# A recurrent attention in chunks: the state held compact, one head on each half of the partitions, and the output in two PSUM banks

## The chip, the cores and the metric

The kernel runs on one core of a Trainium2 chip. Five engines of that core work side by side, each in its own program order: PE (matrix multiplication), with its weight loads shown apart as PEld; DVE (elementwise and reductions); ACT (activations, copies); POOL (elementwise, slower); SP (issues DMAs). PE writes only to PSUM, which has eight banks of 2 KB in each of 128 partitions. An engine waits for another by a semaphore, and whatever stands behind the waiting instruction in its program order waits too.

The metric is the time of one execution on the device in microseconds (us), as the median over runs.

## The reference

Two parts follow one another. The first is a recurrent attention over 768 steps for 4 batches and 8 heads of 48 channels. The second routes the 3072 resulting rows through 8 experts, with weights from a gate that is normalised eight times over rows and columns (Sinkhorn).

```python
state = zeros(B, H, D, D)                         # B, H, S, D = 4, 8, 768, 48
for t in range(S):
    kt, vt, rt = k[:, :, t], v[:, :, t], r[:, :, t]
    cur = einsum('bhd,bhe->bhde', u[None] * kt, vt)
    y[:, :, t] = einsum('bhd,bhde->bhe', rt, state + cur)
    state = w[None, :, :, None] * state + einsum('bhd,bhe->bhde', kt, vt)

x = y as (3072, 384)
P = exp(x @ w_gate - max); eight times: rows of P to sum 1, columns of P to sum N / E
out = sum over e of P[:, e] * (relu(x @ w1[e]) @ w2[e])
```

## The kernel before

The time axis is cut into chunks of 128 steps. There are 24 chunks (`NTT`), six to a batch (`NCHB`); chunk `tt` is number `c = tt % 6` of its batch, and the state is zero ahead of `c = 0`. Within a chunk the recurrence is written as matrix products. r and k are first scaled by powers of the decay w (`rp`, `kp`), transposed on PE (`prT`, `pkT`) and copied by ACT to `rT`, `kT`, with the eight heads as four pairs: head 2p on partitions 0 to 47, head 2p+1 on 64 to 111, the other partitions zero. Then:

- `stage_c`: `pA` = kT times rT for each head, in two PSUM tiles, one for each head of a pair, on quarters of 64x64 of the array. DVE copies the part above the diagonal to `at` with a masked copy (`COPY_PREDICATED`), one for each tile.
- `stage_s` (for c < 5): `pu` = kp times v, the chunk's contribution to the state, on columns of the array 32 wide. DVE adds the old state, POOL multiplies by the chunk's decay `wbd`; for c = 0 DVE multiplies alone. The result is the state of the next chunk.
- `stage_d`: `py` = rT times state (the state part, for c > 0) plus `at` times v. DVE adds the bonus term `av` (the tile `rk`), which gives `x`, and takes the row's greatest value and a scale from it.

The state `S` is a tile of [128, 4 pairs, 2, 48]: for each pair a block of 128 x 96 in which the even head's state stands in the upper left and the odd head's in the lower right; the other two quarters are zero, set once at the start. So one product of 128 rows and 96 columns gives both heads of a pair:

```python
for p_ in range(NPAIR):
    for hs in quarters:
        T.matmul(
            pyp[hs, p_, :], d["rT"][:, p_, hs], d["S"][:, p_].rearrange("p j d -> p (j d)"),
            start=first, stop=False, skip_group_check=True,
        )
```

A product in fp32 runs as two passes, so each call leaves two records in the trace.

The main loop runs over `i` from 0 to 26. Iteration i makes the scaled r and k of chunk i+2 (`prep`), the transposes of chunk i+1 (`stage_b`), `stage_c` and `stage_s` of chunk i, `stage_d` of chunk i-1, the gate's logits of chunk i-3 (`px`, then `lparts`). Between them stand fixed numbers of units of the first expert's products (`ph`, `po`) as soon as these are ready, for i < 5 a few matmuls on zeros (`pz`), and small steps that split weights and combine tokens on DVE, ACT and POOL (`prepare`, `n_steps`). Every engine is kept in the order in which the code issues (`InOrder`, line 29, which is why all lines read L29).

`prT`, `pkT`, the two `pA`, `pu` and `py` share one pool of four PSUM banks (`ps3`, tag "pa"). Each new tile takes over the bank of the tile four places earlier in the order of allocation, and its first matmul waits until that tile has been read. With six tiles in an iteration, `prT` and `pkT` of chunk i+2 take over the banks of the two `pA` of chunk i, and `pu` that of a `prT`. After the attention (near 226 us) the rest of the experts follows, PE almost without a break.

Of the kernel before, what the change touches and what calls it, by code (L numbers as in the profile page):

```python
# [8 lines left out]
F32 = mybir.dt.float32  # L9
# [3 lines left out]
ALU = mybir.AluOpType  # L13
# [19 lines left out]
def rwkv_sinkhorn_moe(  # L33
# [13 lines left out]
    V, S_, G, T, Q = (  # L47
        InOrder(tc, e) for e in (nc.vector, nc.scalar, nc.gpsimd, nc.tensor, nc.sync)
    )

    B, H, S, D = r.shape
    NT, DM = out.shape
    E, _, F = w1.shape
    P = 128
    C = 128
    NPAIR = H // 2
    NCHB = S // C
    NTT = NT // P
# [5 lines left out]
    HP = 64  # L64
    QP = 32
# [63 lines left out]
    def pow2_scale(m, inv, s, down):  # L129
        V.tensor_scalar(inv, m, 1e-30, down, op0=ALU.max, op1=ALU.mult)  # L130
        V.tensor_single_scalar(
            inv.bitcast(I32), inv.bitcast(I32), EXP_MASK, op=ALU.bitwise_and
        )
        V.reciprocal(s, inv)
# [137 lines left out]
    ac = att.enter_context(tc.tile_pool(name="ac", bufs=1))  # L272
    ld = att.enter_context(tc.tile_pool(name="ld", bufs=3))
    at2 = att.enter_context(tc.tile_pool(name="at2", bufs=2))
    ps3 = att.enter_context(tc.tile_pool(name="ps3", bufs=4, space=PSUM))
# [13 lines left out]
    def spin(n):  # L289
        pz = ps2.tile([P, TB], F32, tag="po", name="pz")  # L290
        for _ in range(n):
            T.matmul(pz, zeros[:, :P], zeros, start=True, stop=True)
# [52 lines left out]
    def fill(x_):  # L345
        n = x_.shape[1]
        S_.mul(
            x_.rearrange("p (a q) -> p a q", q=HP),
            unit[:, :1, 1:].broadcast_to([P, n // HP, HP]), 0.0,
        )  # L350

    fill(hbx[:, 2 * HB :])
    spin(19)
    wbd = ac.tile([P, NPAIR, 2, D], F32, name="wbd")
    G.memset(wbd, 0.0)

    mask = ac.tile([P, C], F32, name="mask")
    G.memset(mask, 1.0)
# [7 lines left out]
    kp_ = [ac.tile([P, H, HP], F32, name=f"kp{i}") for i in range(3)]  # L366
    at_ = [ac.tile([P, H, C], F32, name=f"at{i}") for i in range(2)]

    ss_ = [ac.tile([P, NPAIR, 2, D], F32, name=f"S{i}") for i in range(3)]
    for t_ in rp_ + kp_:  # L370
        G.memset(t_[:, :, D:], 0.0)
    for t_ in ss_:
        for j in range(2):
            G.memset(t_[j * HP : (j + 1) * HP, :, 1 - j, :], 0.0)
    fill(at_[0].rearrange("p h c -> p (h c)"))

    rk0 = at2.tile([P, H, D], F32, tag="rk", name="rk_0", bufs=3)
# [88 lines left out]

    wc = ac.tile([P, NPAIR], F32, name="wc")
    V.tensor_tensor(wc, pw[:, :, HP], pw[:, :, HP], op=ALU.mult)
    for j in range(2):
        rows = slice(j * HP, j * HP + D)  # L470
        V.tensor_copy(wbd[rows, :, j, :], wc[rows].unsqueeze(2).broadcast_to([D, NPAIR, D]))
    iswg = ac.tile([P, 1], F32, name="iswg")
    swg = ac.tile([P, 1], F32, name="swg")
    wgm = ac.tile([P, 1], F32, name="wgm")
# [3 lines left out]
    def gate_max():  # L478
        V.tensor_reduce(wgm, wg, axis=AX.XY, op=ALU.max, apply_absolute_value=True)
# [11 lines left out]
    st = {}  # L491
# [4 lines left out]
    def prep(tt):  # L496
        ld_ = loads[tt]
        G.tensor_tensor(rp_[tt % 2][:, :, :D], ld_["r"], rt4, op=ALU.mult)
        V.tensor_tensor(kp_[tt % 3][:, :, :D], ld_["k"], kt4, op=ALU.mult)
        st[tt] = {}  # L500
# [49 lines left out]
    def stage_s(tt):  # L550
        d = st[tt]
        c = tt % NCHB
        if c < NCHB - 1:
            vn = loads[tt]["v"]
            kp = kp_[tt % 3].rearrange("p (a j) d -> p a (j d)", j=2)

            pu = ps3.tile([P, NPAIR, D], F32, tag="pa", name=f"pu_{tt}")
            for p_ in range(NPAIR):
                for q in range(0, P, QP):
                    T.matmul(  # L560
                        pu[q : q + QP, p_, :], kp[:, p_, q : q + QP],
                        vn[:, 2 * p_ + q // HP, :], start=True, stop=True,
                    )
            sn = ss_[tt % 3]
            for j in range(2):
                rows = slice(j * HP, (j + 1) * HP)
                if c == 0:
                    V.tensor_tensor(sn[rows, :, j, :], pu[rows], wbd[rows, :, j, :], op=ALU.mult)
                else:
                    V.tensor_tensor(sn[rows, :, j, :], pu[rows], d["S"][rows, :, j, :], op=ALU.add)  # L570
            if c:
                for j in range(2):
                    rows = slice(j * HP, (j + 1) * HP)
                    G.tensor_tensor(
                        sn[rows, :, j, :], sn[rows, :, j, :], wbd[rows, :, j, :], op=ALU.mult
                    )
            st.setdefault(("S", tt + 1), sn)

    def stage_d(tt):
        d = st[tt]  # L580
        c = tt % NCHB
        vn = loads[tt]["v"]
        at = at_[tt % 2]
        py = ps3.tile([P, H, D], F32, tag="pa", name=f"py_{tt}")
        pyp = py.rearrange("p (a j) d -> p a (j d)", j=2)

        quarters = [slice(q, q + QP) for q in range(0, P, QP)]
        first = True
        if c > 0:
            for p_ in range(NPAIR):  # L590
                for hs in quarters:
                    T.matmul(
                        pyp[hs, p_, :], d["rT"][:, p_, hs], d["S"][:, p_].rearrange("p j d -> p (j d)"),
                        start=first, stop=False, skip_group_check=True,
                    )
                first = False
        for h in range(H):
            for hs in quarters:
                T.matmul(
                    py[hs, h, :], at[:, h, hs], vn[:, h, :],  # L600
                    start=first, stop=(h == H - 1), skip_group_check=True,
                )
            first = False
        x = at2.tile([P, DM], F32, tag="x", name=f"x_{tt}")
        V.tensor_tensor(x, py.rearrange("p h d -> p (h d)"), d["av"].rearrange("p h d -> p (h d)"), op=ALU.add)
        m = at2.tile([P, 1], F32, tag="xm", name=f"xm_{tt}")
        V.tensor_reduce(m, x, axis=AX.X, op=ALU.max, apply_absolute_value=True)
        s = at2.tile([P, 1], F32, tag="xs", name=f"xs_{tt}")
        pow2_scale(m, inv_s[:, tt : tt + 1], s, 0.125)
        d["x"], d["s"] = x, s  # L610
# [8 lines left out]
    def stage_e(tt):  # L619
        Q.dma_start_transpose(xtile(tt), st[tt]["x"].rearrange("p l d -> p (l d)"))  # L620
# [130 lines left out]
    def n_steps(i):  # L751
        return STEPS.get(i, (2, 2) if i < 22 else (3, 2))
# [5 lines left out]
    for i in range(NTT + 3):  # L758
        if i == 1:
            gate_max()  # L760
        if i + 2 < NTT:
            prep(i + 2)
        if i + 1 < NTT:
            bonus_dot(i + 1)
        if i + 1 < NTT and i:
            stage_b(i + 1)
        if 2 <= i <= NTT + 1:
            scale_x(i - 2)
            stage_e(i - 2)
            emitted[0] = i - 1  # L770
        if i + 4 < NTT:
            load_part(i + 4, "r", r)
            load_part(i + 4, "k", k)
            if i == 0:
                load_part(4, "v", v)
                Q.dma_start(raws[1], w2[0].rearrange("(c p) d -> p c d", p=P))
        work(1, i > 4)
        if i < NTT:
            bonus(i)
            if ("S", i) in st:  # L780
                st[i]["S"] = st.pop(("S", i))
            stage_c(i)
            stage_s(i)
        if i == 2:
            gate_split(gate_res)
        if i == 0:
            stage_b(1)
        if i > NTT:
            work(2)
        for _ in range(n_steps(i)[0] if i < 5 else 0):  # L790
            prepare()
        if 1 <= i <= NTT:
            stage_d(i - 1)
            if i + 4 < NTT:
                load_part(i + 4, "v", v)
        for _ in range(n_steps(i)[0] if i >= 5 else 0):
            prepare()
        if 3 <= i:
            stage_f(i - 3, ps2.tile([P, TB], F32, tag="po", name=f"px_{i}"))
        if i <= NTT:  # L800
            work(2 if i > 8 else 1, i > 4)
        if i == 1:
            gate_res = gate_across()
        for _ in range(n_steps(i)[1]):
            prepare()
        done = i - 2
        if 0 <= done < NTT and done % TH == TH - 1:
            po_ = done // TH
            if po_ == 0:
                units += [g1_unit(0, fc, W) for fc in range(FC)]  # L810
                units += [g2_half(0, t, 0, W) for t in range(TH)]
                pend = [(0, t, 1) for t in range(TH)]
            for j in range(2 if po_ else 0):
                g1 = [g1_unit(po_, fc, W) for fc in range(j * FHC, (j + 1) * FHC)]
                g2 = [g2_half(*a, W) for a in pend]
                units += merged(g1, g2)
                pend = [(po_, t, j) for t in range(TH)]
# [151 lines left out]
    _, singles2, _, high2, low2 = early[2]  # L969
# [249 lines left out]
    for s in range(NS):  # L1219
        tasks = stage_tasks(s)  # L1220
        for g in range(NG):
            for j in range(2):
                for n, nxt in enumerate(g1_slots(s, g, j)):
# [3 lines left out]
                    i = j * NPR + n  # L1227
# [37 lines left out]
```

## Time and profile before

| what | value |
|---|---|
| median of 3 runs | 1535.79 us (1535.17, 1535.79, 5633.4) |
| the profiled execution: its own time | 1534.0 us |
| its span, first to last instruction | 1532.5 us |
| mean granted PE clock | 0.997 |
| 0 to 88 us: PE, DVE, POOL busy | 70.5, 80.1, 68.8 us; clock 0.96 |
| 88 to 226 us: PE, DVE, POOL busy | 136.0, 119.1, 124.1 us of 138; clock 0.99 |
| 226 us to the end: PE, DVE, POOL busy | 1301.6, 834.1, 404.6 us of 1306.5; clock 1.00 |

One of the three runs took 5633.4 us; the median does not see it. In the profile, "PE prT <- DVE at: 4.7, 3, 3.2" means that PE stood idle ahead of work on prT until DVE had done something with at: 4.7 us in all, 3 times, 3.2 at the longest. A group's line gives the engine, the operation, output <- inputs, the tile of the array, the shape, the count, then busy us and the mean ns of one. Of matmuls that run side by side on parts of the array the busy time counts the overlap once. In the timeline, records of one kind that follow each other are merged: start, length from the first start to the last end, count, and in brackets the idle time before and what ended it.

### The profile page before, as it was taken

How to read it: one execution, taken by the hardware profiler on the slowest of the kernel's cores; microseconds unless marked ns; L12 is line 12 of the kernel's file. 1: busy time of each engine (PE TensorE's matmuls, PEld its weight loads, DVE VectorE, ACT ScalarE, POOL GpSimd, SP SyncE). 2: the span in 40 equal slices, each digit the busy share in tenths (PEclk: the TensorE clock that was granted, in tenths of full speed). 3: DMA queues.
4: the chain of work that ended last, by engine and by line, in shares of the span. 5: the costliest groups of instructions: out<-in, count | busy, mean ns of one | idle time of the engine just before them, and what ended most of it. 6: DMA issues, size and time to landing. Idle time of an engine off the chain costs nothing.

```text
span 1532.5 us, 29056 instructions
## 1 busy us (share of the span) xinstructions
PE 1508.2 (98%) x11721; PEld 850.5 (55%) x11721; DVE 1033.3 (67%) x1714; ACT 662.2 (43%) x1168; POOL 597.5 (39%) x708
## 2 busy tenths in 40 slices
PE   7899999999999999999999999999999999999999
PEld 4667766655555555555555555555555555555555
DVE  8988887676666666667666666656666566566564
ACT  4333434435354444535454444535344444445320
POOL 8779995120213425242424334242424224242200
PEclk9999999999999999999999999999999999999999
DMA  9665623121235665665656665655445554555433
GB/s 203 96 112 116 134 58 109 47 76 52 98 57 107 91 115 86 126 94 91 107 90 128 92 123 80 127 62 98 59 67 86 60 98 57 99 59 99 57 93 130
DMA packets 186859, 143.31 MB, mean 94 GB/s; under 512 B 109537, under 2 KB 180962, under 8 KB 186722
## 3 DMA queue, kind: packets, MB, share of 16 engines
q0 software_dynamic: 44928, 61.36, 32.4%
q1 hardware_dynamic: 141584, 80.07, 20.2%
q8 instruction: 92, 1.51, 0.4%
q14 instruction: 45, 0.37, 0.1%
q10 hardware_dynamic: 210, 0.00, 0.0%
HBM read 55.39 MB, written 80.23 MB: 88 GB/s over the span
## 4 chain that ended last, share of the span: by engine, by line
PE 92%; DVE 5%; POOL 1%; issue 1%; ACT 0%; DMA 0%; DVEq 0%; POOLq 0%; another core or an unknown queue 0%; ACTq 0%
PE po L29 48%; PE bZ L29 12%; PE bY L29 12%; PE bA L29 5%; PE ph L29 5%; PE bB L29 5%; PE bC L29 2%; PE py L29 1%; PE pA L29 1%; POOL rk L29 1%; DVE at L29 1%; DVE hb L29 1%; DVE ws L29 0%; PE prT L29 0%; PE pu L29 0%
## 5 line engine op out<-in xcount | busy, mean ns | idle before, releaser
L29 PE MATMUL po<-ws,hbx 128*128 128x384 f16 x3360 | 736.8, 326 | 0.0
L29 POOL DMA_DIRECT2D accd<-stg x288 | 250.0, 868 | 695.0 <-ACT stg L29 676.5
L29 PEld LDWEIGHTS <-hbx 128*128 128x128 f16 x3504 | 334.2, 98 | 292.9
L29 PEld LDWEIGHTS <-ws 128*128 128x128 f16 x3096 | 302.0, 98 | 245.6 <-issue 3.0
L29 ACT ACTIVATE hbx<-tb 128x512 f16<-128x512 f32 x224 | 141.0, 630 | 450.7 <-DVE tb L29 450.7
L29 PE MATMUL po<-ws,hb 128*128 128x384 f16 x1248 | 323.4, 326 | 3.6 <-DVE ws L29 2.3
L29 DVE TENSOR_TENSOR tb<-bY,tb 128x512 f32<-128x512 f32 x168 | 116.2, 692 | 195.6 <-PE bY L29 195.4
L29 ACT ACTIVATE stg<-po,pe 128x384 f32<-128x384 f32 x312 | 179.4, 575 | 121.8 <-PE po L29 98.7
L29 PE MATMUL bZ<-xv,ws 128*128 128x512 f16 x840 | 227.0, 379 | 0.7 <-DVE tb L29 0.7
L29 PE MATMUL bY<-xv,ws 128*128 128x512 f16 x840 | 227.0, 379 | 0.0
L29 DVE TENSOR_TENSOR tb<-bZ,tb 128x512 f32<-128x512 f32 x168 | 115.5, 688 | 136.5 <-PE bZ L29 136.5
L29 PEld LDWEIGHTS <-hb 128*128 128x128 f16 x1248 | 121.4, 98 | 97.2 <-issue 4.2
L29 POOL TENSOR_TENSOR ucb<-rawb 128x256 f32<-128x256 f32 x84 | 75.9, 954 | 118.5 <-DMA rawb<-in_moe_w_dram 118.5
L29 DVE TENSOR_TENSOR tb<-bB,tb 128x512 f32<-128x512 f32 x112 | 77.5, 692 | 48.8 <-PE bB L29 46.9
L29 PE MATMUL ph<-hbx,ws 128*128 128x384 f16 x576 | 105.1, 328 | 0.6 <-DVE hb L29 0.6
L29 DVE SCALAR_TENSOR_TENSOR hb<-tb,hbx 128x512 f16<-128x512 f32 x112 | 77.1, 689 | 24.7 <-ACT hbx L29 19.5
L29 PE MATMUL bA<-xv,ws 128*128 128x512 f16 x336 | 90.8, 379 | 0.0
L29 PE MATMUL bB<-xv,ws 128*128 128x512 f16 x336 | 90.8, 379 | 0.0
L29 DVE SCALAR_TENSOR_TENSOR hbx<-tb,hbx 128x512 f16<-128x512 f32 x112 | 78.2, 698 | 14.7 <-ACT hbx L29 10.4
L29 ACT ACTIVATE hb<-ph 128x384 f16<-128x384 f32 x64 | 31.3, 491 | 73.9 <-PE ph L29 73.5
L29 ACT COPY tb<-bZ 128x512 f32<-128x512 f32 x56 | 32.8, 586 | 65.5 <-PE bZ L29 65.5
L29 ACT COPY stg<-po 128x384 f32<-128x384 f32 x48 | 22.9, 478 | 75.7 <-PE po L29 60.5
(166 smaller groups left out, 1537.7 us busy)
## 6 DMA issues: line engine op xcount, KB each, us to landing
accd<-stg POOLq DMA_DIRECT2D x288, 192.0 KB, 3.7
rawb<-in_moe_w_dram SPq DMA_DIRECT2D x28, 768.0 KB, 7.0
e0d<-stg SPq DMA_DIRECT2D x48, 192.0 KB, 2.1
hb<-e0d SPq DMA_DIRECT2D x48, 192.0 KB, 3.7
vn<-in_v_dram SPq DMA_DIRECT2D x24, 192.0 KB, 4.2
accd<-stg SPq DMA_DIRECT2D x24, 192.0 KB, 1.8
accd<-hb POOLq DMA_DIRECT2D x24, 192.0 KB, 4.8
rawb<-accd SPq DMA_DIRECT2D x24, 192.0 KB, 2.4
```

What stands on the lines that cost most here:

```text
L29: return lambda *a, **k: self.tc.keep_in_program_order(f(*a, **k))
```

## The change

Four edits go together.

1. The state tile becomes [128, 4 pairs, 48]: the even head's state on partitions 0 to 63, the odd head's on 64 to 127, without the zero quarters. `wbd` shrinks likewise. The additions and multiplications of the state, two over 64 partitions each, become one over 128. The memsets of the zero quarters and of `wbd` go.
2. The state part of y (`state_part`, new) runs on quarters of 64x64 of the array, 48 columns each, where it ran on 128x32 with 96 columns. The number of matmuls stays 16 in a chunk.
3. y stands in two PSUM tiles, `py_0` for the even and `py_1` for the odd heads, each of [128, 4, 48]. The addition that makes x becomes two.
4. `stage_s` of chunk i moves behind `stage_d` of chunk i-1; the state part comes straight behind `stage_c`.

```diff
-    wbd = ac.tile([P, NPAIR, 2, D], F32, name="wbd")
-    G.memset(wbd, 0.0)
+    wbd = ac.tile([P, NPAIR, D], F32, name="wbd")
...
-    ss_ = [ac.tile([P, NPAIR, 2, D], F32, name=f"S{i}") for i in range(3)]
+    ss_ = [ac.tile([P, NPAIR, D], F32, name=f"S{i}") for i in range(3)]
...
-    for t_ in ss_:
-        for j in range(2):
-            G.memset(t_[j * HP : (j + 1) * HP, :, 1 - j, :], 0.0)
...
-    for j in range(2):
-        rows = slice(j * HP, j * HP + D)
-        V.tensor_copy(wbd[rows, :, j, :], wc[rows].unsqueeze(2).broadcast_to([D, NPAIR, D]))
+    V.tensor_copy(wbd, wc.unsqueeze(2).broadcast_to([P, NPAIR, D]))
...
             sn = ss_[tt % 3]
-            for j in range(2):
-                rows = slice(j * HP, (j + 1) * HP)
-                if c == 0:
-                    V.tensor_tensor(sn[rows, :, j, :], pu[rows], wbd[rows, :, j, :], op=ALU.mult)
-                else:
-                    V.tensor_tensor(sn[rows, :, j, :], pu[rows], d["S"][rows, :, j, :], op=ALU.add)
-            if c:
-                for j in range(2):
-                    rows = slice(j * HP, (j + 1) * HP)
-                    G.tensor_tensor(
-                        sn[rows, :, j, :], sn[rows, :, j, :], wbd[rows, :, j, :], op=ALU.mult
+            if c == 0:
+                V.tensor_tensor(sn, pu, wbd, op=ALU.mult)
+            else:
+                V.tensor_tensor(sn, pu, d["S"], op=ALU.add)
+                G.tensor_tensor(sn, sn, wbd, op=ALU.mult)
+            st.setdefault(("S", tt + 1), sn)
+
+    def y_banks(tt):
+        return [ps3.tile([P, NPAIR, D], F32, tag="pa", name=f"py_{tt}_{g}") for g in range(2)]
+
+    def state_part(tt):
+        d = st[tt]
+        if tt % NCHB == 0:
+            return
+        d["py"] = y_banks(tt)
+        for p_ in range(NPAIR):
+            for g in range(2):
+                rows = slice(g * HP, (g + 1) * HP)
+                for hs in (slice(0, HP), slice(HP, C)):
+                    T.matmul(
+                        d["py"][g][hs, p_, :], d["rT"][rows, p_, hs], d["S"][rows, p_, :],
+                        start=(p_ == 0), stop=False, skip_group_check=True,
...
+        pys = d["py"] if "py" in d else y_banks(tt)
         for h in range(H):
-            for hs in quarters:
+            for q in range(0, P, QP):
                 T.matmul(
-                    py[hs, h, :], at[:, h, hs], vn[:, h, :],
-                    start=first, stop=(h == H - 1), skip_group_check=True,
+                    pys[h % 2][q : q + QP, h // 2, :], at[:, h, q : q + QP], vn[:, h, :],
+                    start=(c == 0 and h < 2), stop=(h >= H - 2), skip_group_check=True,
...
-        V.tensor_tensor(x, py.rearrange("p h d -> p (h d)"), d["av"].rearrange("p h d -> p (h d)"), op=ALU.add)
+        xv = x.rearrange("p (a g d) -> p g a d", g=2, d=D)
+        av = d["av"].rearrange("p (a g) d -> p g a d", g=2)
+        for g in range(2):
+            V.tensor_tensor(xv[:, g], pys[g], av[:, g], op=ALU.add)
...
             stage_c(i)
-            stage_s(i)
+        if 1 <= i <= NTT:
+            state_part(i - 1)
...
             stage_d(i - 1)
+        if i < NTT:
+            stage_s(i)
+        if 1 <= i <= NTT:
```

What the change does to the order is seen on PE around chunk 14 (iteration 14). The names carry running numbers; pA_1 is the second of the two tiles of stage_c, py's inputs are S with rT (the state part) or vn with at, and px belongs to the gate. On PE before, from the last pA on:

```order
L29 MATMUL pA_1_2582<-rT_2375,kT_2382 64x128 x2
L29 MATMUL pu_2601<-vn_1972,kp_170 32x48 x16
L29 MATMUL py_2622<-S_173,rT_2192 32x96 x16
L29 MATMUL py_2622<-vn_1781,at_172 32x48 x32
L29 LDWEIGHTS hbx
L29 MATMUL px_2681<-wgp,hbx 128x16
```

On PE now, first the start of the state part behind the last pA, with the engines that an instruction waits for:

```order
L29 MATMUL pA_1_2579<-rT_2372,kT_2379 64x128 x2
L29 MATMUL py_0_2598<-S_172,rT_2188 64x48 [waits Activation_49]
L29 MATMUL py_0_2598<-S_172,rT_2188 64x48
L29 MATMUL py_1_2599<-S_172,rT_2188 64x48 [waits Activation_49]
L29 MATMUL py_1_2599<-S_172,rT_2188 64x48
```

and then the end of y, with pu:

```order
L29 MATMUL py_1_2599<-vn_1775,at_171 32x48 x4
L29 MATMUL pu_2657<-vn_1966,kp_169 32x48 [waits DVE_49]
L29 MATMUL pu_2657<-vn_1966,kp_169 32x48 x15
L29 LDWEIGHTS hbx [waits DMAHW2_49,DMASW3_49]
L29 MATMUL px_2678<-wgp,hbx 128x16
```

pu has moved from ahead of y to behind it, and it waits for DVE. With seven tiles in an iteration, pu takes over the bank of the same chunk's first pA, which DVE's masked copy reads; pkT of chunk i+2 takes over that of py_0.

On DVE, chunk 13 before; at is what the masked copies write, and x, xm, inv_s, xs are the output, its greatest value and its scale:

```order
L29 COPY_PREDICATED at_172<-mask,pA_0_2408 128x4x128
L29 COPY_PREDICATED at_172<-mask,pA_1_2409 128x4x128
L29 TENSOR_TENSOR S_174<-pu_2428,S_173 64x4x48 x2
L29 TENSOR_TENSOR x_2482<-py_2449,rk_2016 128x384
L29 TENSOR_REDUCE xm_2484<-x_2482 128x1
```

and now:

```order
L29 COPY_PREDICATED at_171<-mask,pA_0_2405 128x4x128
L29 COPY_PREDICATED at_171<-mask,pA_1_2406 128x4x128
L29 TENSOR_TENSOR x_2459<-py_0_2425,rk_2010 128x4x48
L29 TENSOR_TENSOR x_2459<-py_1_2426,rk_2010 128x4x48
L29 TENSOR_REDUCE xm_2462<-x_2459 128x1
L29 TENSOR_SCALAR inv_s<-xm_2462 128x1
L29 TENSOR_SCALAR inv_s<-inv_s 128x1
L29 RECIPROCAL xs_2464<-inv_s 128x1
L29 TENSOR_TENSOR S_173<-pu_2468,S_172 128x192
```

The state's addition has moved from ahead of x to behind x's scale, and there are two additions for x and one for the state.

More of the change, by code (lines that the diff above doesn't have):

```diff
@@ L564, in stage_s @@
             sn = ss_[tt % 3]
-            for j in range(2):
-                rows = slice(j * HP, (j + 1) * HP)
-                if c == 0:
-                    V.tensor_tensor(sn[rows, :, j, :], pu[rows], wbd[rows, :, j, :], op=ALU.mult)
-                else:
-                    V.tensor_tensor(sn[rows, :, j, :], pu[rows], d["S"][rows, :, j, :], op=ALU.add)
-            if c:
-                for j in range(2):
-                    rows = slice(j * HP, (j + 1) * HP)
-                    G.tensor_tensor(
-                        sn[rows, :, j, :], sn[rows, :, j, :], wbd[rows, :, j, :], op=ALU.mult
+            if c == 0:
[18 more added lines that the diff above has]
+                        start=(p_ == 0), stop=False, skip_group_check=True,
                     )
-            st.setdefault(("S", tt + 1), sn)
     def stage_d(tt):
@@ L583, in stage_d @@
         at = at_[tt % 2]
[L584 to L590, printed above, removed]
-                for hs in quarters:
[L592 to L596, printed above, removed]
+        pys = d["py"] if "py" in d else y_banks(tt)
         for h in range(H):
-            for hs in quarters:
+            for q in range(0, P, QP):
                 T.matmul(
-                    py[hs, h, :], at[:, h, hs], vn[:, h, :],
-                    start=first, stop=(h == H - 1), skip_group_check=True,
+                    pys[h % 2][q : q + QP, h // 2, :], at[:, h, q : q + QP], vn[:, h, :],
+                    start=(c == 0 and h < 2), stop=(h >= H - 2), skip_group_check=True,
                 )
-            first = False
         x = at2.tile([P, DM], F32, tag="x", name=f"x_{tt}")
-        V.tensor_tensor(x, py.rearrange("p h d -> p (h d)"), d["av"].rearrange("p h d -> p (h d)"), op=ALU.add)
+        xv = x.rearrange("p (a g d) -> p g a d", g=2, d=D)
+        av = d["av"].rearrange("p (a g) d -> p g a d", g=2)
+        for g in range(2):
+            V.tensor_tensor(xv[:, g], pys[g], av[:, g], op=ALU.add)
         m = at2.tile([P, 1], F32, tag="xm", name=f"xm_{tt}")
```

## The prediction, on record before the changed kernel ran

> **What bounds the kernel now.** I read the page first, then the busy time by stretches, then the groups by shape, and last the timeline of single chunks on PE, DVE and ACT. The page's head gives the span and the share of each engine:
>
> ```profile
> span 1532.5 us, 29056 instructions
> PE 1508.2 (98%) x11721; PEld 850.5 (55%) x11721; DVE 1033.3 (67%) x1714; ACT 662.2 (43%) x1168; POOL 597.5 (39%) x708
> ```
>
> PE is idle for 24 us of the whole span, so almost anything that PE saves or loses shows at the end. Where the idle time lies is seen in the stretches (busy us and instructions of PE, PEld, DVE, ACT, POOL, then the granted clock):
>
> ```profile
> 40.00:60.00 20.00, 16.22 (x386) 11.49 (x379) 19.50 (x36) 4.62 (x9) 15.39 (x17) 0.89 0.51 94
> 60.00:80.00 20.00, 17.21 (x457) 12.81 (x459) 18.12 (x45) 9.63 (x17) 13.87 (x16) 1.00 0.80 110
> 80.00:100.00 20.00, 16.77 (x321) 11.82 (x309) 18.70 (x34) 5.29 (x11) 12.47 (x14) 0.91 0.52 109
> 100.00:120.00 20.00, 20.00 (x462) 14.64 (x464) 15.20 (x32) 7.39 (x15) 19.38 (x22) 1.00 0.81 126
> 500.00:1000.00 500.00, 500.00 (x2734) 267.37 (x2733) 329.43 (x502) 239.65 (x422) 184.85 (x223) 1.00 0.64 104
> ```
>
> Two regimes: until about 88 us DVE is busy 18 to 19.5 of 20 us and sets the pace, while PE waits; from 100 us PE is full. The attention ends near 226 us, and the change touches nothing behind that. PE's waits in the first regime, with their last releaser (us, times, longest):
>
> ```profile
> PE prT L29 <- DVE at L29: 4.7, 3, 3.2
> PE po L29 <- DVE ws L29: 2.3, 1, 2.3
> PE prT L29 <- POOL rp L29: 0.5, 1, 0.5
> ```
>
> The second row is the last large one. So the change is worth two things: what it does to DVE before 88 us, and what it does to PE in the later chunks.
>
> **The state part.** One chunk on PE, in order of time, then the groups by shape that the change edits:
>
> ```profile
> 154.45 1.10 PE L29 MATMUL pA<-rT,kT 64*64 64x128 f32 x32
> 155.48 0.55 PE L29 MATMUL pu<-vn,kp 128*32 128x48 f32 x32
> 155.84 0.84 PE L29 MATMUL py<-S,rT 128*32 128x96 f32 x32
> 156.50 0.89 PE L29 MATMUL py<-vn,at 128*32 128x48 f32 x64
> 157.33 0.30 PE L29 MATMUL px<-wgp,hbx 128*128 128x16 f16 x6
> ...
> L29 PE MATMUL py<-S,rT 128*32 128x96 f32 x640 | 17.9, 255 | 0.0
> L29 DVE TENSOR_TENSOR x<-py,rk 128x384 f32<-128x384 f32 x24 | 13.3, 555 | 1.2 <-PE py L29 0.7
> L29 DVE TENSOR_TENSOR S<-pu,S 64x192 f32<-64x192 f32 x32 | 11.1, 347 | 0.5
> L29 POOL TENSOR_TENSOR S<-S,wbd 64x192 f32<-64x192 f32 x32 | 21.7, 679 | 1.2
> ```
>
> From start to start, the state part takes 156.50 - 155.84 = 0.66 us: 32 records, four at a time, 8 steps of 82 ns for 96 columns. pu, with 48 columns, takes 0.36 us, 45 ns a step. The new state part also has 32 records, four at a time, of 48 columns, but on tiles of 64x64 as pA has. From below it costs what pu does, 0.36. From above: pA takes 1.03 us, 129 ns a step for 128 columns; taking off 80 columns at (82-45)/48 = 0.77 ns leaves 67 ns, 0.54 us; and if 64-wide loads set the pace whatever the columns, 1.03 us stays. I take 0.42, nearer to pu because its shape in columns is the same: 0.24 us saved a chunk (0.30 to 0.12, or 0.37 lost). By the Trainium skill (TensorEngine Tiling (Array Packing), Instruction Overhead) a matmul with fewer than about 60 columns costs what one of 60 does; by that the part would take 0.66 x 60/96 = 0.41 us and save 0.25, and the 45 ns of pu against 82 (0.55, not 0.62) do not show such a floor.
>
> 20 of the 24 chunks have a state part, which PE does one iteration later. Those of chunks 1 to 5 and 7 lie before 88 us, where PE has time to spare; there it gains nothing. 14 remain.
>
> **DVE.** The two state additions of a chunk become one over 128 partitions with the same 192 elements each: 0.35 us less. The output's addition becomes two of 192 elements. No row has 128x192 from PSUM; the nearest is 64x192 at 0.35, so 2 x 0.35 against 0.555: 0.15 more (0 to 0.2). Before 88 us there are 8 of each: -8 x 0.35 + 8 x 0.15 = -1.6 us, and that moves the point where PE is let go. Bounds: -2.8 if the halves cost nothing more, and 0 if PE's own later waits fill the time.
>
> **POOL and start.** Sixteen pairs of multiplications by the decay become single ones, some 0.6 us less each, but POOL now gets them later, since the state addition stands behind the output's scale on DVE. PE waits for POOL only 0.5 us in all (the row above), and the state is needed one iteration later, so zero; if that cover went, POOL's order would put rp late by one such wait. The dropped memsets and one copy lie ahead of waits that stay:
>
> ```profile
> POOL rp L29 <- ACT rtab L29: 3.8, 1, 3.8
> DVE kp L29 <- ACT ktab L29: 1.2, 1, 1.2
> ```
>
> Zero as well. PE's work in the new order (y, then pu) has the same changes of tile shape as before.
>
> **The new wait.** A chunk now takes seven PSUM tiles out of four banks where it took six. The bank of pu is therefore the one that pA's first half had, and pu cannot start before DVE has done the first masked copy of the same chunk (the order shows pu waiting for DVE, before for ACT). Before, PE went on past pu, y, px and one or two units of expert work until the next prT. Now only the state part and the rest of y (0.42 + 0.83 us) stand between pA and that wait; behind pu queue px, the units and the next transposes, all of PE. In chunks where DVE is late this costs at once. Chunk 13, and chunk 19, which is built alike (both follow a chunk with zero state, so there is no state part between):
>
> ```profile
> 127.13 1.10 PE L29 MATMUL pA<-rT,kT 64*64 64x128 f32 x32
> 128.17 0.55 PE L29 MATMUL pu<-vn,kp 128*32 128x48 f32 x32
> 128.53 0.86 PE L29 MATMUL py<-vn,at 128*32 128x48 f32 x64
> 129.33 0.30 PE L29 MATMUL px<-wgp,hbx 128*128 128x16 f16 x6
> 134.67 2.11 PE L29 MATMUL po<-ws,hb 128*128 128x384 f16 x12 [0.74 <-DVE lparts L29]
> ...
> 125.32 0.83 ACT L29 CAST xv<-ws 128x768 f16<-128x768 f32 x1
> 126.19 1.11 DVE L29 TENSOR_TENSOR xv<-ws,xv 128x768 f16<-128x768 f32 x1 [1.96 <-ACT xv L29]
> 130.72 1.34 DVE L29 COPY_PREDICATED at<-mask,pA 128x512 f32<-128x512 int32 x2
> ...
> 182.22 0.55 PE L29 MATMUL pu<-vn,kp 128*32 128x48 f32 x32
> 182.59 0.86 PE L29 MATMUL py<-vn,at 128*32 128x48 f32 x64
> 183.38 0.30 PE L29 MATMUL px<-wgp,hbx 128*128 128x16 f16 x6
> 184.63 1.35 DVE L29 COPY_PREDICATED at<-mask,pA 128x512 f32<-128x512 int32 x2
> ```
>
> In chunk 13 PE would reach pu at 128.17 + 0.80 = 128.97; the first of the two copies ends at 130.72 + 0.67 = 131.39: 2.4 us. DVE is late there because a cast on ACT came late (the 1.96), and the cast follows PE's own work, so the lateness moves with PE. The wait takes over the 0.74 at 134.67, so net 1.7. In chunk 19: 182.22 + 0.79 = 183.01 against 184.63 + 0.68 = 185.31, 2.3 us. Chunk 12 shows the other kind:
>
> ```profile
> 119.31 0.55 PE L29 MATMUL pu<-vn,kp 128*32 128x48 f32 x32
> 119.84 1.39 DVE L29 COPY_PREDICATED at<-mask,pA 128x512 f32<-128x512 int32 x2
> ```
>
> PE at 119.31 + 0.42 + 0.82 = 120.55, the copy done at 120.54: no wait, but no slack either, so in such a chunk a shorter state part only waits. I therefore count the 0.24 in 8 of the 14 chunks: -1.9 us. The waits of the other chunks behind 13 and 19 I put at 0.8, between 0 (PE is already late by then) and 1.7 (one more net wait like chunk 13's).
>
> **Sum.** -1.6 - 1.9 + 1.7 + 2.3 + 0.8 = +1.3 us. The profiled execution took 1534.0 us (span 1532.5, and 1.5 around it); that makes 1535.3. The median of the three runs shown is 1535.79, 1.8 above it; in its terms 1537.1, rounded to 1537.
>
> **The rivals.**
> - The wait doesn't bite. DVE does 0.2 us less in each chunk and may run early enough, then only the gains stay: 1535.8 - 1.6 - 14 x 0.24 = 1530.8, and 1528.8 with both low prices (2.8 and 14 x 0.30). For it: DVE has 15.2 of 20 us at 100. Against it: chunk 13's lateness comes from ACT, not from DVE's load.
> - The wait is paid nearly everywhere (slower). If every second of the 20 pu's pays chunk 13's 2.4 us, 24 less the gains of 3.5 gives 1556; from 15 of them on it is past 2% ((30.7 + 3.5) / 2.4 = 14.3). For it: DVE is nearly full in 80 to 100 us. Against it: chunk 12, and that a PE that waited once comes later the next time.
> - The clock. After a wait of 3.19 us PE ran slow; a unit of 9 that takes 1.63 us took 2.68:
>
> ```profile
> 50.64 0.72 PE L29 MATMUL prT<-ident,rp 128*128 128x128 f32 x4 [3.19 <-DVE at L29]
> 52.30 2.68 PE L29 MATMUL ph<-hbx,ws 128*128 128x384 f16 x9
> 59.92 1.63 PE L29 MATMUL ph<-hbx,ws 128*128 128x384 f16 x9
> ```
>
>  The stretch 80 to 100 with a mean clock of 0.91 lost 0.09 x 20 = 1.8 us. One or two such stretches behind chunks 13 and 19 make 1539 to 1541. The Trainium skill (TensorE: Matmul & The Clock Gate, Part 1: The HAM clock gate) says that the clock halves after an idle window of about 3.4 us that runs free of the kernel. By that rule my waits of 2.4 us may or may not fall so, which the trace neither shows nor excludes.
> - The tiles of 64x64 don't get shorter with fewer columns (the change doesn't do what it says): 14 x 0.37 = 5.2 lost, and with the waits' 4.8 less the 1.6 of DVE 8.4 in all, 1544.
>
> **How the numbers follow.** Forecast 0.35, no bite 0.25, the clock 0.20, paid widely 0.12, long tiles 0.08. About 2% (30.7 us) is what a measurement of this kernel can tell from no change; only the end of the widely paid case passes it, 0.02, and on the fast side the gains together stay far below it, 0.01. So 0.97 for within 2%. The range runs from 1529, the low end of the first rival, to 1546, which cuts off most of the widely paid case: some 0.15 left out, beside what I have not thought of.
>
> **What would show it.** The groups: py<-S at 64x48 with about 9 us busy instead of 17.9; S additions 20, x additions 48, at about 0.35 us each. The waits: pu <- DVE at, in chunks 13 and 19 above 2 us. The stretches: PE no longer full in 120 to 140 and 180 to 200, and let go before 88 us. It would be wrong if pu shows no wait, if a stretch behind 226 us changes, or if the copies move with PE in most chunks.

## The result and the profile after

| | changed kernel | kernel before |
|---|---|---|
| median | 1543.92 us (5 runs, 1542.9 to 1547.83) | 1535.61 us (5 runs, 1535.17 to 1535.79 and one of 5633.4) |
| profiled execution: its own time, span | 1543.92, 1542.4 us | 1534.0, 1532.5 us |
| ratio | 1.0066, 95% interval 1.0055 to 1.0077 | |

So the change made the kernel 0.66% slower, about 8 us: within 2%, inside the range, 7 us above the forecast of 1537.0. The head of the page of the changed kernel:

```profile
span 1542.4 us, 29007 instructions
PE 1509.8 (98%) x11721; PEld 850.3 (55%) x11721; DVE 1029.0 (67%) x1717; ACT 661.3 (43%) x1168; POOL 584.8 (38%) x685
```

PE is busy as long as before, within 2 us; the span is 10 us longer, so most of the loss is idle time of PE. Where it lies is seen in the stretches of the changed kernel (columns as in the prediction: busy us and instructions of PE, PEld, DVE, ACT, POOL, then granted clock, where 1.00 is full speed, DMA share, GB/s):

```profile
120.00:140.00 20.00, 17.53 (x379) 12.64 (x379) 15.20 (x29) 7.22 (x14) 17.99 (x19) 1.00 0.46 94
140.00:160.00 20.00, 17.91 (x428) 13.06 (x416) 18.33 (x37) 6.76 (x13) 12.27 (x13) 1.00 0.61 124
...
180.00:200.00 20.00, 16.52 (x329) 11.53 (x327) 13.53 (x25) 7.14 (x14) 17.03 (x20) 0.91 0.43 96
200.00:220.00 20.00, 18.21 (x307) 12.42 (x311) 15.04 (x32) 6.78 (x13) 9.47 (x11) 0.91 0.21 41
```

Before, PE was busy 19.26, 20.00, 20.00 and 19.30 us in these four, at a clock of 1.00. Now 9 to 17% of a stretch is idle, and the last two ran at a mean clock of 0.91, which is 1.8 us lost in each (0.09 x 20). From 226 us to the end PE idled 4.9 us before and idles 4.5 us now, at a clock of 1.00 in both. PE's waits in the changed kernel (us, times, longest) name one releaser:

```profile
PE pu L29 <- DVE at L29: 20.9, 14, 2.5
...
PE prT L29 <- DVE at L29: 0.5, 1, 0.5
```

The wait of prT that stood at 4.7 us has gone to pu and has grown more than fourfold. On PE's timeline of the changed kernel, pu with its idle time in brackets, and the units of expert work behind it:

```profile
130.86 0.55 PE L29 MATMUL pu<-vn,kp 128*32 128x48 f32 x32 [2.47 <-DVE at L29]
...
188.12 0.85 PE L29 MATMUL pu<-vn,kp 128*32 128x48 f32 x32 [2.00 <-DVE at L29]
189.09 2.85 PE L29 MATMUL ph<-hbx,ws 128*128 128x384 f16 x9
...
200.42 0.55 PE L29 MATMUL pu<-vn,kp 128*32 128x48 f32 x32 [1.89 <-DVE at L29]
201.06 3.26 PE L29 MATMUL po<-ws,hb 128*128 128x384 f16 x12
204.12 2.20 PE L29 MATMUL ph<-hbx,ws 128*128 128x384 f16 x9
```

130.86 is chunk 13, 188.12 chunk 19, 200.42 chunk 20. A unit of nine matmuls (`ph`) takes 1.63 us elsewhere and 2.85 behind chunk 19's wait; a unit of twelve (`po`) takes 2.11 elsewhere and 3.26 behind chunk 20's: two stretches at half clock (the granted clock is 0.50 from 189 to 191 and from 202 to 205 us), which the kernel before does not have behind 100 us. The waits of chunks 14, 15 and 16 were 1.36, 0.56 and 0.43 us, so behind 100 us there are 8.7 us of such waits, and within chunk 21's pu PE waits 1.37 us more for something that the profile does not name. The other 12.2 of the 20.9 us lie ahead of 100 us. What they do there is seen at the start of pA in chunk 12: first in the kernel before, then in the changed kernel, then in the version with six tiles of the next section, which has only 0.4 us of these waits:

```profile
118.28 1.10 PE L29 MATMUL pA<-rT,kT 64*64 64x128 f32 x32
...
117.61 1.10 PE L29 MATMUL pA<-rT,kT 64*64 64x128 f32 x32
...
114.40 1.10 PE L29 MATMUL pA<-rT,kT 64*64 64x128 f32 x32
```

Nearly without the waits PE is there 3.2 us sooner than with them.

DVE shows why chunk 20 waited as well:

```profile
125.53 1.15 DVE L29 TENSOR_TENSOR xv<-ws,xv 128x768 f16<-128x768 f32 x1 [2.16 <-ACT xv L29]
...
195.21 1.78 DVE L29 TENSOR_TENSOR xv<-ws,xv 128x768 f16<-128x768 f32 x1 [2.16 <-ACT xv L29]
```

Each time DVE idles 2.16 us for ACT's cast. ACT stands behind a copy of PE's own output (the copy at 193.97 idles 1.50 us for PE's po, the cast follows at 194.34), so when PE comes late, ACT and with it DVE's masked copy come late too: here the wait of chunk 19 bought chunk 20 no slack.

The groups that the change edits, in the changed kernel:

```profile
L29 PE MATMUL py<-S,rT 64*64 64x48 f32 x640 | 13.0, 217 | 0.1
L29 DVE TENSOR_TENSOR x<-py,rk 128x192 f32<-128x192 f32 x48 | 14.6, 345 | 0.4 <-PE py L29 0.4
L29 POOL TENSOR_TENSOR S<-S,wbd 128x192 f32<-128x192 f32 x16 | 13.3, 833 | 17.6 <-DVE S L29 17.6
```

The state part fell from 17.9 to 13.0 us busy, not to 9. POOL now waits 17.6 us for DVE's state addition (before 1.2), which made a second suspect. Chunk 18 is one in which PE did not wait:

```profile
175.54 1.10 PE L29 MATMUL pA<-rT,kT 64*64 64x128 f32 x32
176.46 0.63 PE L29 MATMUL py<-S,rT 64*64 64x48 f32 x32
177.02 0.89 PE L29 MATMUL py<-vn,at 128*32 128x48 f32 x64
177.73 0.54 PE L29 MATMUL pu<-vn,kp 128*32 128x48 f32 x32
178.20 0.30 PE L29 MATMUL px<-wgp,hbx 128*128 128x16 f16 x6
```

From pA to px it takes 2.66 us, where chunk 16 took 2.88 before (154.45 to 157.33): the work itself is 0.22 us shorter.

### The profile page after: what moved, and what is told of

Same layout as the page of the kernel before. It is cut to its first block, busy times and chain, and to the rows that moved or that the text cites. A ratio compares the mean times of both kernels' runs of the same rounds, so it can differ in the third digit from the quotient of the medians.

```text
span 1542.4 us, 29007 instructions
## 1 busy us (share of the span) xinstructions
PE 1509.8 (98%) x11721; PEld 850.3 (55%) x11721; DVE 1029.0 (67%) x1717; ACT 661.3 (43%) x1168; POOL 584.8 (38%) x685
## 4 chain that ended last, share of the span: by engine, by line
PE 89%; DVE 6%; issue 1%; DMA 1%; SPq 1%; ACT 1%; POOL 0%; DVEq 0%; ACTq 0%
PE po L29 47%; PE bZ L29 12%; PE bY L29 12%; PE bA L29 5%; PE bB L29 5%; PE ph L29 5%; PE bC L29 2%; DVE at L29 1%; DVE kp L29 1%; SPq L29 1%; DVE ws L29 1%; PE py L29 1%; DVE xsc L29 1%; PE pu L29 1%; DVE hb L29 0%
## 5 line engine op out<-in xcount | busy, mean ns | idle before, releaser
L29 DVE SCALAR_TENSOR_TENSOR hb<-ph,hb 128x384 f16<-128x384 f32 x64 | 35.4, 553 | 38.0 <-ACT hb L29 37.0
```

The costliest lines, as they stand in the source:

```text
L29: return lambda *a, **k: self.tc.keep_in_program_order(f(*a, **k))
```

## The experiments

Three theories were put to the test. Theory 1: the seventh PSUM tile makes PE wait at pu. Theory 2: the state's addition, moved behind the output's scale, comes too late. Theory 3: the new state part or the second x addition costs more than it saves. All ratios are against the kernel before, run on the same chip.

| run | what it is | median us | ratio (95% interval) |
|---|---|---|---|
| e1_six_tiles | changed, pu in py_0's bank | 1527.87 | 0.9958 (0.9944 to 0.9971) |
| e2_late_state_only | before, stage_s late | 1535.27 | 1.0004 (0.9995 to 1.0013) |
| e3_seven_tiles_early_state | changed, stage_s early | 1546.04 | 1.0075 (1.0061 to 1.0089) |
| e4_six_tiles_early_state | six tiles, stage_s early | 1530.49 | 0.9971 (0.9959 to 0.9983) |
| after_again | changed | 1542.88 | 1.0045 (1.0033 to 1.0058) |
| e5_filled_waits | changed, four waits filled | 1541.12 (6 runs, one of 4205.73) | 1.0040 (1.0027 to 1.0052) |
| e7_half_columns | e1, half of the state's columns left out of y | 1527.99 (1 run) | |
| e9_state_first_on_dve | e1, state addition ahead of x | 1526.72 | 0.9949 (0.9936 to 0.9962) |
| e11_seven_tiles_late_pu | changed, pu behind two units | 1528.01 | 0.9950 (0.9937 to 0.9964) |
| e1_again | e1 | 1527.93 | 0.9948 (0.9935 to 0.9962) |
| e9_again | e9 | 1528.44 | 0.9958 (0.9944 to 0.9971) |

**Six tiles.** pu stands in the free half of py_0's bank. So that neither waits for the other's reader, the matmuls of y and pu are issued first and DVE's additions behind them. Of the edit, the lines that give pu its place:

```diff
...
-        return [ps3.tile([P, NPAIR, D], F32, tag="pa", name=f"py_{tt}_{g}") for g in range(2)]
+        two = ps3.tile([P, 2, NPAIR, D], F32, tag="pa", name=f"py_{tt}_0")
+        st[tt]["pu"] = two[:, 1]
+        return [two[:, 0], ps3.tile([P, NPAIR, D], F32, tag="pa", name=f"py_{tt}_1")]
...
```

> The changed kernel with one thing undone: pu no longer takes a PSUM tile of its own but stands in the free half of py_0's bank, so a chunk takes six tiles out of four banks again. The order on PE and DVE stays that of the changed kernel (pu behind y, the state's addition behind the output's scale). Theory 1 (the seventh tile makes PE wait at pu for DVE's masked copy; the 8.7 us of such waits behind 100 us and the two half-clock stretches behind them are the whole loss): the waits pu <- DVE at fall from 20.9 us to below 3, no half-clock stretch near 188 and 202 us, and the time is 1530 to 1534 us, 0.1 to 0.35% below the kernel before. Theory 2 (the state's addition stands too late on DVE, POOL waits for it): nothing of that is touched, 1540 us or more. Theory 3 (the state part on quarters or the second x addition costs more than it saves): also 1540 or more.

It took 1527.87 us, 0.42% below the kernel before: theories 2 and 3 expected 1540 or more. Its wait for at is back where it was before the change, and about as long (PE's waits of this run):

```profile
PE prT L29 <- DVE at L29: 3.9, 4, 1.3
```

No stretch behind 100 us has a clock below 1.00. The order of both engines is the changed kernel's; only a bank differs.

**The late state alone.** In the kernel before, `stage_s` is moved:

```diff
             stage_c(i)
-            stage_s(i)
...
             stage_d(i - 1)
+        if i < NTT:
+            stage_s(i)
...
```

> The kernel before with one part of the change alone: pu and the state's addition and multiplication stand behind y and the output's scale, as in the changed kernel. State tile, state part and the one y tile are those of before, six PSUM tiles in a chunk. Theory 1: no wait of PE comes from it, so it stays within 1.5 us of the kernel before, though POOL waits for DVE's state addition as long as in the changed kernel (17.6 us). Theory 2: the loss is here, 4 us or more above the kernel before. Theory 3: as theory 1.

The ratio is 1.0004: theory 2 falls. One part of the expectation missed: POOL waited 6.4 us for the state addition, not 17.6 (POOL's waits of this run, then of the first run):

```profile
POOL S L29 <- DVE S L29: 6.4, 7, 1.2
```

```profile
POOL S L29 <- DVE S L29: 7.6, 6, 2.6
```

So the moved order accounts for 6 to 8 of the 17.6 us, and the rest comes with the seventh tile. The first run beats the kernel before with 7.6 us of it, the last run of this section is as fast with 16.7 us of it, and the run with the state early, next, has none of it and is the slowest of all: this wait of POOL costs nothing.

**Seven tiles with the state early.** The fourth edit undone alone, and then with six tiles:

```diff
             stage_c(i)
+            stage_s(i)
...
-        if i < NTT:
-            stage_s(i)
...
```

> The changed kernel with its fourth edit undone alone: pu and the state's addition stand ahead of y as before; seven tiles in a chunk stay. By the order of allocation py_1 now takes over the bank of the first pA. Theory 1: the wait moves to py_1, which PE reaches 0.8 us sooner than it reached pu, so each wait that bites is longer by some 0.8 us: the time is that of the changed kernel or up to 6 us more (1542 to 1550), with waits of PE py <- DVE at in place of pu <- DVE at. Theory 2: with the state's addition early again the loss goes, 1532 to 1538 us. Theory 3: unchanged, 1541 to 1546 us, without a longer wait.

> Both undone: six tiles (pu in the free half of py_0's bank) and pu ahead of y as before, the state's addition on DVE ahead of x. Compact state, 64x64 state part, y in two banks stay. Theories 1 and 2 both expect 1530 to 1534 us; with the first run it tells whether the place of the state's addition is worth anything: theory 1 expects no more than 1 us between the two, theory 2 several. Theory 3: 1540 us or more.

With seven tiles it took 1546.04 us, and the wait moved to the other tile (PE's waits of that run):

```profile
PE py L29 <- DVE at L29: 19.6, 16, 2.9
```

Theory 1 said so; that each wait would grow by 0.8 held in chunk 19 (2.90 for 2.00) and not in chunk 13 (1.64 for 2.47). With six tiles it took 1530.49, faster than before, as expected, but by the medians 2.6 us slower than the first run (single runs: 1528.78 to 1530.84 against 1527.34 to 1529.51). Theory 1 had allowed 1 us; theory 2 had expected the opposite sign. Chunk 18 on PE's timeline of the six-tile run shows where they go (pu's matmuls are named py<-vn,kp here, since they share its tile):

```profile
169.38 1.10 PE L29 MATMUL pA<-rT,kT 64*64 64x128 f32 x32
170.41 0.55 PE L29 MATMUL py<-vn,kp 128*32 128x48 f32 x32
170.89 0.68 PE L29 MATMUL py<-S,rT 64*64 64x48 f32 x32
171.50 0.89 PE L29 MATMUL py<-vn,at 128*32 128x48 f32 x64
172.32 0.30 PE L29 MATMUL px<-wgp,hbx 128*128 128x16 f16 x6
```

It takes 2.94 us from pA to px, where the changed kernel's order takes 2.66 and the kernel before 2.88. The same five groups run in both; what differs is how often the tile's shape changes. With pu ahead the array goes from 64x64 to 128x32, back to 64x64 and to 128x32 again; with the state part straight behind pA it changes once. Two changes more cost 0.28 us in this chunk, and 0.24 to 0.31 against the first run in the other chunks behind 86 us that have pu and a state part and no wait. The Trainium skill (TensorEngine Tiling (Array Packing), Key Properties) says that a change of the tiling mode drains the engine; by these rows, 0.14 us for each. So the state part's saving exists only together with the fourth edit: with pu ahead of it, 2.94 us is even 0.06 more than before the change.

**The place on DVE.** To hold PE's order and DVE's apart, the first run's kernel with the state's addition ahead of x:

```diff
-        if 1 <= i <= NTT:
-            stage_d_add(i - 1)
         if i < NTT:
             stage_s_add(i)
         if 1 <= i <= NTT:
+            stage_d_add(i - 1)
```

> The first run's kernel (six tiles, pu behind y on PE) with the state's addition ahead of x on DVE instead of behind the output's scale. In the first run PE waited 1.0 us once for DVE's S and POOL waited long for it. If the place of that addition is worth anything, 1 to 2 us less than the first run (0.9948 to 0.9953 of the kernel before); if the gap between the first and the fourth run came of PE's order alone (the state part straight behind pA, without a change of tile shape between), it stays within 1 us of the first run (0.9952 to 0.9965).

> The first run's kernel again (six tiles, pu and the state's addition behind y), as the yardstick for the next run on one chip: 0.9945 to 0.997 of the kernel before.

> The kernel with the state's addition ahead of x on DVE again, beside the first run's kernel on one chip. If the place of that addition on DVE is worth anything, 1 to 2 us below the run before; if not, within 0.7 us.

In its own first run this kernel took 1526.72 us, 1 us less than the first one had on another chip; side by side on one chip it took 1528.44 against 1527.93 us, within 0.7. The addition's place on DVE is worth nothing that can be measured here. From the kernel with pu ahead it differs in PE's order, not in DVE's, and there the pair from pA to px stands at

```profile
165.94 1.10 PE L29 MATMUL pA<-rT,kT 64*64 64x128 f32 x32
...
168.58 0.31 PE L29 MATMUL px<-wgp,hbx 128*128 128x16 f16 x6
```

It is 2.64 us. So the 2.6 us come from PE's order.

**What sets the state part's length.** The first run's kernel with half of the columns:

```diff
-    d["py"][g][hs, p_, :], d["rT"][rows, p_, hs], d["S"][rows, p_, :],
+    d["py"][g][hs, p_, : D // 2], d["rT"][rows, p_, hs], d["S"][rows, p_, : D // 2],
```

> The first run's kernel (six tiles) with the state part over the first 24 of the 48 columns only; the second half of the state is left out of y. Disputed is what sets the 0.56 us of the 64x64 state part (8 steps of four records, 58 ns each where PE's timeline shows 1.03 us for the first step after a change of tile shape). If the loads of the 64-wide weights set it, start to start stays at 0.5 to 0.56 us and pA to px at 2.6 us. If the columns do, it falls to about 0.3 us and pA to px to 2.4.

On its timeline:

```profile
150.07 1.10 PE L29 MATMUL pA<-rT,kT 64*64 64x128 f32 x32
151.00 0.61 PE L29 MATMUL py<-S,rT 64*64 64x24 f32 x32
151.54 0.89 PE L29 MATMUL py<-vn,at 128*32 128x48 f32 x64
```

It takes 0.54 us from start to start with 24 columns, 0.56 with 48. Between these two the columns do not set it. The loads of 64-wide weights could (a load of that group takes 134 ns on average, one of the 32-wide group before 115), and so could a least time of the matmul itself; no run changed the loads' width alone.

**The clock.** The changed kernel once more, and with matmuls on zeros in the time that PE waits in chunks 13, 14, 19 and 20:

```diff
...
+        if i in FILL:
+            bank_ = ps2.tile([P, TB], F32, tag="po", name=f"px_{i}")
+            for _ in range(FILL[i]):
+                T.matmul(bank_[:, 2 * HP :], zeros[:, :P], zeros[:, 2 * HP :], start=True, stop=True)
         if i < NTT:
             stage_s(i)
...
```

> The changed kernel once more, on the chip of the next run, so that the two can be set side by side. Theory 1: 0.55 to 0.8% above the kernel before, the two half-clock stretches near 188 and 202 us again, since the same waits stand ahead of them; if such stretches fall at random they stand elsewhere or are missing.

> The changed kernel with matmuls on zeros (128x384, about 0.18 us each, into the free columns of the bank that px uses next) ahead of pu in chunks 13, 14, 19 and 20: 12, 6, 10 and 9 of them, a little less than PE waits there. PE still cannot start pu earlier. If idle time of PE is what brings the half-clock stretches at 188 and 202 us, the slices 180 to 220 us show a clock of 1.00, the waits at those four places shrink below 0.6 us each, and the time is 2.5 to 4.5 us below the changed kernel on the same chip, while pu starts as late after pA as before. If the stretches come of something else (of the work, or of chance), they stay and the time is within 1 us of the changed kernel.

In the repeated run of the changed kernel the half-clock stretches stood behind chunks 13 and 19, not 19 and 20:

```profile
131.06 0.55 PE L29 MATMUL pu<-vn,kp 128*32 128x48 f32 x32 [2.48 <-DVE at L29]
131.70 3.10 PE L29 MATMUL po<-ws,hb 128*128 128x384 f16 x12
...
201.74 0.55 PE L29 MATMUL pu<-vn,kp 128*32 128x48 f32 x32 [1.76 <-DVE at L29]
202.38 2.11 PE L29 MATMUL po<-ws,hb 128*128 128x384 f16 x12
```

So each stood behind one of the three longest waits behind 100 us, two of three in either profile, and which two is not fixed. With the waits filled (0.43, 0.27, 0.28 and 0.71 us of them were left, below 0.6 was expected), no such stretch stood there (stretches of that run, clock in the column behind POOL):

```profile
120.00:140.00 20.00, 19.57 (x391) 13.61 (x384) 15.18 (x31) 7.23 (x14) 17.95 (x20) 1.00 0.49 101
...
180.00:200.00 20.00, 19.20 (x354) 13.10 (x352) 14.98 (x29) 7.15 (x14) 18.83 (x21) 1.00 0.46 103
200.00:220.00 20.00, 19.40 (x453) 14.19 (x454) 17.27 (x39) 6.78 (x13) 11.49 (x13) 1.00 0.25 51
```

By its whole time the run does not separate from the changed kernel (1.0040 against 1.0045, and 1.9 us between the medians without the run of 4205.73, where 2.5 to 4.5 were expected; single runs of the changed kernel lie between 1540.2 and 1544.1). By the stage it does. From the start of pA in chunk 12 to that in chunk 23 PE took 105.8 us, against 109.6 and 108.9 in the two profiles of the changed kernel and 98.4 in the kernel before. Of the 3.1 to 3.7 us given back, the two chunks with a half-clock stretch bring 1.3 to 1.7 each; 1.3 more come from chunk 21, whose wait without a releaser (1.37 and 1.01 us) is missing here, and later waits that grow again take some of it back. 7.4 us remain. In this profile PE reaches chunk 12 later by 0.7 us than in the repeated one (118.54 against 117.80), with four stretches of 20 us at 0.91 ahead of it where the other has one at 0.83. This is one profile with filled waits, so it makes idle time the likely cause and does not exclude chance. The Trainium skill (TensorE: Matmul & The Clock Gate, Part 1: The HAM clock gate) describes a window of about 3.4 us that runs free of the kernel; that waits of 1.8 to 2.5 us were followed by half clock in one run and not in the other agrees with the free phase, but they are shorter than the window, and no run here shows what inside a window decides.

**Seven tiles, more work ahead of the wait.** If it is not the tile but the short way from pA to pu, seven tiles must be harmless where pu comes later:

```diff
...
-        if i < NTT:
-            stage_s(i)
...
             work(2 if i > 8 else 1, i > 4)
+        if i < NTT:
+            stage_s(i)
...
```

> The changed kernel, seven tiles in a chunk as it has, with stage_s (pu and the state's addition) moved once more: behind px and the two units of expert work, 4 us of PE's work further from the masked copy it depends on. Theory 1 in a sharper form (the seventh tile costs because only 1.3 us of PE's work stands between pA and the wait on its copy, not because of the tile or the bank as such): the waits pu <- DVE at fall below 3 us in all, no half-clock stretch behind 100 us, 1527 to 1534 us, unless the second pA of the next chunk, which takes the bank of pu, now waits for the later state addition (up to 4 us, 1538). If seven tiles cost wherever pu stands, 1541 us or more.

1528.01 us, ratio 0.9950: as fast as with six tiles. PE's waits of this run, then chunk 13 on its timeline:

```profile
PE pu L29 <- DVE at L29: 5.3, 4, 1.8
```

```profile
123.04 1.10 PE L29 MATMUL pA<-rT,kT 64*64 64x128 f32 x32
...
125.06 2.11 PE L29 MATMUL po<-ws,hb 128*128 128x384 f16 x12
127.00 1.63 PE L29 MATMUL ph<-hbx,ws 128*128 128x384 f16 x9
128.56 0.55 PE L29 MATMUL pu<-vn,kp 128*32 128x48 f32 x32
```

pu starts 5.5 us behind pA and does not wait. No stretch behind 100 us has a clock below 1.00. The 5.3 us (below 3 were expected) lie ahead of 50 us, where PE has no units of expert work to put in between. Theory 1 stands in this sharper form.

## Why the prediction came out as it did

The result lay inside the range and on the forecast side of 2%, but that the sum came out so small is partly luck: two errors of opposite sign hid in it. The gains were taken too small and the waits much too small. What the change would be worth without the waits is measured by the versions without them: 0.9948 to 0.9958, 6 to 8 us faster. The waits and what follows them therefore cost about 15 us, not 4.8. The two profiles agree: the spans of the changed kernel and of the first run differ by 15.5 us, of which 3.2 lie ahead of chunk 12 and 12.3 between chunk 12 and chunk 23 (109.6 against 97.3); the 12.3 come to as much as the 8.7 of named waits and twice 1.8 at half clock.

- **Bound and place.** Right in the main: PE lost what was lost, in the stretches named and in 140 to 160, and nothing changed behind the attention. That PE would lose ahead of chunk 12 too was not foreseen.
- **The new wait in chunks 13 and 19.** Right in place and size: 2.4 and 2.3 us forecast, 2.47 and 2.00 measured.
- **The waits of the other chunks, 0.8 us.** This is the term that failed. Chunks 14, 15, 16, 20 and 21 waited 1.36, 0.56, 0.43, 1.89 and 1.37 us, 5.6 in all (the last without a named releaser). The reason given was that a PE that is late already finds the copy done. The subtraction made for chunks 13 and 19 could have been made for every chunk; rows of the kernel before, PE's and then DVE's, for chunks 15 and 20, with the copy of chunk 16 between:

```profile
145.59 1.10 PE L29 MATMUL pA<-rT,kT 64*64 64x128 f32 x32
...
189.39 1.10 PE L29 MATMUL pA<-rT,kT 64*64 64x128 f32 x32
```

```profile
148.50 1.33 DVE L29 COPY_PREDICATED at<-mask,pA 128x512 f32<-128x512 int32 x2
...
157.91 1.33 DVE L29 COPY_PREDICATED at<-mask,pA 128x512 f32<-128x512 int32 x2
...
192.63 1.33 DVE L29 COPY_PREDICATED at<-mask,pA 128x512 f32<-128x512 int32 x2
```

  By chunk 18 above, PE reaches pu 2.19 us behind pA, so at 147.78, 156.64 (pA at 154.45) and 191.58; the first copies end 0.67 behind their starts, at 149.17, 158.58 and 193.30: 1.4, 1.9 and 1.7 us. Chunks 14, 21 and 22 give 0.6, 1.3 and 1.0 in the same way, all together with 13 and 19 12.6 us, where 8.7 and the unnamed 1.4 were measured: some single waits shrink as PE falls behind (chunks 15 and 16), others do not, and the sum falls by a fifth. Chunk 12, from which the prediction read "no wait, but no slack either", was no pattern for those behind it.
- **DVE before 88 us, -1.6.** Not seen in the changed kernel: PE reaches chunk 12 0.7 us sooner than before (117.61 for 118.28), and all of that comes from the start of the program, where the prediction had zero. The 12.2 us of waits that lie ahead of 100 us, which the prediction did not price, stand against it. Without them (the first run) the lead at chunk 12 is 3.9 us. From start to start on DVE the pair of state additions took 0.75 us and the single one takes 0.25, so 0.50 is saved, not 0.35; x takes 0.65 for 0.59, so 0.06 more, not 0.15. The mean duration of an instruction overstates what the next one waits. Eight chunks of that would be 3.5 us. But PE does not show it chunk by chunk: at chunk 8 the first run is only 0.3 us ahead (77.77 for 78.04), and by chunk 10 it is 3.5 ahead (96.92 for 100.42). Between the two PE's wait for ws is 1.0 us shorter (1.31 for 2.28), and the half-clock stretch that the kernel before has there (0.91 in 80 to 100, 1.8 us) is missing. How much of the 3.9 is DVE's shorter work and how much the place of that stretch stays open.
- **The state part, 0.24 a chunk.** Right: 0.22 measured from pA to px, and the changes of tile shape are as many as before, as the prediction said. The change has only moved. Before, it stood behind pA, which took 1.03 us and now takes 0.92, so it costs 0.11, near the 0.14 above; now it stands behind the state part, whose 0.56 us from start to start has it in. By itself the part takes about 0.45 us, an estimate (0.56 - 0.11), where 0.42 was taken. The upper bound's reason, a pace that does not depend on the columns, is what the run with half of them showed; its price of 1.03 was pA's, too far. The 0.41 that followed from the Trainium skill (TensorEngine Tiling (Array Packing), Instruction Overhead: a matmul of few columns costs as much as one of about 60) is close to this estimate too, and 24 columns costing what 48 do agrees with such a floor.
- **The rivals.** None came alone. The clock was no alternative to the waits but their sequel, two stretches, as priced. "Paid nearly everywhere" was right in its count (14 waits) and wrong in the 2.4 us each (20.9 / 14 = 1.5). "The wait doesn't bite" is what the runs without the wait show: 1531 forecast, or 1529 with both low prices, and 1528 measured.
- **POOL, zero.** Held, although the wait shown is 17.6 us; seven tiles with the late pu have 16.7 us of it and are as fast as six tiles.

## What to carry to other kernels

Count the tiles of a pool against its buffers whenever a change adds one, find the instruction that inherits the earliest-read bank, and compare, for every iteration of the old trace, when its engine would arrive with when the reader ends; a wait is cured as well by work placed ahead of it (seven tiles, 0.9950) as by one tile fewer (0.9948 to 0.9958). Group matmuls of one tile shape, and price a saved elementwise instruction by starts, not by its duration. Where an engine feeds the one it waits for, being late buys little slack.

## What was not expected of the hardware

- Two more changes of the tile's shape cost 0.28 us in a chunk of 2.66, more than the whole new state part saved (0.22).
- The state part on 64x64 takes 0.56 us with 48 columns and 0.54 with 24.
- Behind 100 us, after idle times of PE of 1.8 to 2.5 us, a half-clock stretch followed in four cases of six in the two profiles of the changed kernel and cost about 1.8 us each; the same idle times filled with matmuls on zeros had none, in one profile.
- Some waits of PE at y and pu, 2.3 us in five places of the first run, have no releaser in the profile; what they are stays open.
